# The first block's diagonal as a product with the identity, in a linear-attention and two-layer kernel

## The chip, the cores and the metric

The kernel runs on one NeuronCore of a Trainium2 chip. The metric is the device time of one execution in microseconds (us). The engines are named as in the profile: PE is TensorE (matrix products), PEld its weight loads, DVE is VectorE, ACT is ScalarE, POOL is GpSimd, SP is SyncE, which issues nearly all transfers.

## The reference

```python
def _attn_ref(r, k, v, w, u):            # B, H, S, D = 4, 8, 768, 48
    for t in range(S):
        cur = np.einsum('bhd,bhe->bhde', u[None] * kt, vt)
        y[:, :, t] = np.einsum('bhd,bhde->bhe', rt, state + cur)
        state = w[None, :, :, None] * state + np.einsum('bhd,bhe->bhde', kt, vt)

def _moe_ref(x, w_in, w_out, alpha):      # x is y as (3072, 384); d_ff = 2048
    h = x @ w_in
    g = np.maximum(h, 0.0) + alpha * np.minimum(h, 0.0)
    return g @ w_out

def _moe2_ref(x, w_in, w_out):            # same sizes
    h = x @ w_in
    sp = np.where(h > 20.0, h, np.log1p(np.exp(np.minimum(h, 20.0))))
    return (h * np.tanh(sp)) @ w_out
```

Token t of a sequence sees the decayed state of the tokens before it, and itself through the bonus u: the coefficient of its own v is the sum over d of r·u·k, one number for each head and token.

## The kernel before

The sequence of 768 tokens is cut into six blocks of 128, for each of the four batch entries. Block 0 is worked out in four whole units, 0 to 3, one for each batch entry; there is no state yet, so the output of a unit is (its masked matrix of scores, with the coefficients on the diagonal) times v. The later blocks go in half units with a carried state (units 4 to 23). As soon as block 0 of all four batch entries stands in the tile `x`, the first layer starts: `mA_h s` makes a 128x512 tile h of hidden slot s (9 matrix products of 512 columns, each fp32 factor split into a high and a low part of type fp32r), `mA_g`, `mA_hi`, `mA_lo` make the activation and split it on ACT and DVE, and `mA_out s` adds it to the three output banks (9 more). There are 96 such slots, 16 for each block; a `batch` (the attention of a half unit) is slipped in at every fourth slot or so. The second layer follows with another 96 slots.

The order on every engine is written out: each piece of work is entered with a number of the table `PLACES`, all pieces are sorted by it, and each engine executes its share strictly in that order. An engine that waits for one instruction holds up all behind it. The transfers are issued by SP in the same order, each waiting for the eighth one before it.

The work ahead of slot 0, unit by unit (u is 0 to 3; the tile with r and k is w8u, w10u, w12u, w14u, the one with k and v w9u, w11u, w13u, w15u):

- `m_first` and `prep_rk` (DVE): the product r·k, and r and k scaled by the decay table RK.
- `c_first` (PE, then a copy by ACT into the tile cc): the coefficients.
- `preset_first`: fills the tile A with the coefficients on its diagonals and zeros elsewhere. For units 0, 1 and 2 this is a select on POOL (L439), for unit 3 eight scaled copies of the identity on ACT (L437).
- `scores` (PE, L458): 32 products into two banks "sc", shared by all units. `masked` (DVE, L462): copies the scores that lie above the diagonal into A, one half at a time.
- `attend0` (PE, L473): A times v, into the unit's output bank (yt, acc or h). `x_first` (ACT) and `x_first_lo` (DVE) split the output into the high and the low part of `x`.
- `keep_warm` (PE, L597): products of zeros into a bank that nobody reads; eight at the start and ten single ones between the units.
- `table_Kn` makes a table of decays from RK, `prep_kn` (POOL) scales k by it, `states_first` makes the first state. `half_tables` (POOL) rewrites the mask columns of the constants tile for the half units once block 0 has used them.
- For units 4 and 5: `prep_c` and `prep_c2` make the coefficients (POOL, then a sum on DVE), `prep_pair` (DVE, L382) scales r and k by RKs, which is RK moved by a transfer, `preset` and `masked` fill the matrix Ah.
- `w_scale`, `w_join`, `w_hi`, `w_lo`: unpack a slot's weights (ACT, DVE, ACT, DVE or POOL). Slot 1's high weights go into the tile that RK stands in.

Of the kernel before, what the change touches and what calls it, by code (L numbers as in the profile page):

```python
# [54 lines left out]
def more_state(u):  # L55
# [6 lines left out]
    "load_unit 2": -124.1803, "load_unit 3": -121.8174, "pad_v 1": -119.5623, "m_first 0": -118.998,
    "c_first 0": -117.2355, "dma_start#": -115.5868, "more_raw 3": -115.5854, "memset": -115.5721,
    "load_k 1": -115.4582, "tensor_scalar": -115.426, "dma_start##": -115.3727, "pad_v 0": -115.2759,
    "load_k 2": -115.0763, "load_k 0": -114.1881, "prep_rk 0": -113.5294, "keep_warm 3####": -111.4759,
# [7 lines left out]
    "m_first 3": -99.4133, "load_RKs": -98.9853, "scores 1": -98.8978, "prep_rk 3": -98.7566, "more_raw 7": -97.9969,  # L73
    "preset_first 1": -97.8327, "attend0 0": -97.7559, "preset_first 2": -97.6565, "w_join (0,0)": -97.4588,
    "c_first 3": -97.3694, "masked 1 0": -97.0636, "masked 1 1": -97.0296, "keep_warm 3###": -96.9282,
    "keep_warm 3#########": -96.6439, "w_hi (0,0) False": -96.6418, "prep_kn 1": -96.5019, "keep_warm 3#": -96.4984,
# [983 lines left out]
```

## Time and profile before

| | before |
|---|---|
| median of 3 runs | 872.95 us (871.37 to 873.61) |
| the profiled execution | 871.12 us |
| its span, first to last instruction | 869.4 us |
| granted TensorE clock | 1.000 |
| PE busy | 860.9 us (99%) |
| DVE busy | 631.2 us |
| ACT busy | 616.1 us |
| POOL busy | 103.7 us |

The span is what the trace covers; 1.72 us of the profiled execution lie outside it. Busy times are sums over the span; PE's includes the products of zeros. One slot of the first layer is 18 products of about 0.227 us, 4.08 us.

### The profile page before, as it was taken

The numbers are of one execution on the slowest core, as the hardware profiler recorded it, in microseconds if no ns is written. First come the engines' busy times: TensorE is split into PE (matmuls) and PEld (weight loads), VectorE is DVE, ScalarE is ACT, GpSimd is POOL, SyncE is SP. The second block draws the span as 40 slices with busy tenths as digits, with TensorE's granted clock in tenths as the row PEclk, the third lists the DMA queues.
The fourth block names the chain that finished last, engine by engine and source line by source line (L and its number), as shares of the span: only waits on it lengthen the run. The fifth ranks groups of instructions, "written<-read, shape, count | busy, mean of one in ns | idle before, by whom it ended". The sixth has DMA issues, their size and how long they took to land.

```text
span 869.4 us, 16713 instructions
## 1 busy us (share of the span) xinstructions
PE 860.9 (99%) x6380; PEld 711.8 (82%) x6380; DVE 631.2 (73%) x1013; ACT 616.1 (71%) x1174; POOL 103.7 (12%) x121
## 2 busy tenths in 40 slices
PE   9999999999999999999999999999999999999998
PEld 6777888888888888888888888888888888888897
DVE  7788865657656565554666887887887887887876
ACT  3797755454455545445555998998998998998886
POOL 4744222111122111100002000000000000000000
PEclk9999999999999999999999999999999999999999
DMA  8977455254344426211620300110110110100101
GB/s 316 278 220 213 111 187 147 77 180 152 130 135 141 139 88 214 70 56 64 214 82 31 110 1 1 26 48 1 26 48 1 25 50 0 27 12 1 26 12 37
DMA packets 65840, 80.41 MB, mean 92 GB/s; under 512 B 39712, under 2 KB 52960, under 8 KB 65760
## 3 DMA queue, kind: packets, MB, share of 16 engines
q1 hardware_dynamic: 65200, 79.24, 30.0%
q8 instruction: 50, 0.82, 0.4%
q14 instruction: 30, 0.25, 0.1%
q10 hardware_dynamic: 560, 0.10, 0.1%
HBM read 61.16 MB, written 15.73 MB: 88 GB/s over the span
## 4 chain that ended last, share of the span: by engine, by line
PE 91%; DMA 4%; ACT 2%; SPq 1%; DVE 1%; issue 0%; POOL 0%; ACTq 0%; DVEq 0%; POOLq 0%
PE h L239 43%; PE acc L644 21%; PE sc L765 8%; PE acc L765 8%; PE yt L765 4%; PE acc L763 3%; DMA rk<-in_rkT 1%; DMA wrawr<-in_w 1%; PE sc L763 1%; PE sc L458 1%; PE h L489 1%; DMA w15u<-in_nat 1%; DMA nat<-in_nat 1%; PE yt L510 1%; PE sc L503 1%; PE yt L489 1%
## 5 line engine op out<-in xcount | busy, mean ns | idle before, releaser
L239 PE MATMUL h<-x,w 128*128 128x512 f32 x1728 | 415.9, 390 | 1.9 <-DVE x L164 1.0
L239 PEld LDWEIGHTS h<-x,w 128*128 128x128 f32 x1728 | 323.8, 188 | 71.2 <-DVE w L164 1.7
L644 PE MATMUL acc<-ghi,w 128*128 128x512 f32 x516 | 175.2, 394 | 0.0
L612 ACT ACTIVATE m<-h 128x512 f32<-128x512 f32 x96 | 57.3, 597 | 87.6 <-PE h L239 87.5
L644 PEld LDWEIGHTS acc<-ghi,w 128*128 128x128 f32 x516 | 96.8, 188 | 21.3
L614 DVE SCALAR_TENSOR_TENSOR g<-m,oma,h 128x512 f32<-128x512 f32 x96 | 71.7, 746 | 57.7 <-ACT m L612 56.6
L161 ACT ACTIVATE ghi<-g 128x512 fp32r<-128x512 f32 x86 | 54.3, 631 | 76.1 <-PE acc L644 46.1
L644 PE MATMUL acc<-glo,w 128*128 128x512 f32 x258 | 100.5, 389 | 0.0
L164 DVE TENSOR_TENSOR glo<-g,ghi 128x512 fp32r<-128x512 f32 x86 | 60.2, 701 | 51.8 <-ACT ghi L161 51.7
L702 DVE SCALAR_TENSOR_TENSOR a<-ghi,h 128x512 f32<-128x512 f32 x96 | 66.1, 688 | 37.8 <-ACT ghi L699 31.3
L702 DVE SCALAR_TENSOR_TENSOR g<-s,c 128x512 f32<-128x512 f32 x95 | 66.7, 702 | 22.7 <-ACT s L699 20.7
L710 ACT ACTIVATE m<-h 128x512 f32<-128x512 f32 x96 | 56.4, 588 | 35.0 <-PE h L239 35.0
L164 DVE TENSOR_TENSOR gloB<-g,ghiB 128x512 fp32r<-128x512 f32 x105 | 72.1, 686 | 6.8 <-ACT ghiB L161 6.8
L699 ACT ACTIVATE ghi<-m,biases 128x512 f32<-128x512 f32 x96 | 69.6, 725 | 3.2
L161 ACT ACTIVATE ghiB<-g 128x512 fp32r<-128x512 f32 x105 | 64.8, 617 | 8.8 <-PE acc L644 6.9
L699 ACT ACTIVATE glo<-ghi,biases 128x512 f32<-128x512 f32 x96 | 68.1, 709 | 0.1
L699 ACT ACTIVATE s<-glo,biases 128x512 f32<-128x512 f32 x96 | 68.1, 709 | 0.0
L699 ACT ACTIVATE s<-s,biases 128x512 f32<-128x512 f32 x96 | 68.0, 708 | 0.0
L765 PE MATMUL sc<-ghiB,w 128*128 128x512 f32 x192 | 66.9, 389 | 0.0
L702 DVE SCALAR_TENSOR_TENSOR b<-ghi,a 128x512 f32<-128x512 f32 x96 | 65.8, 685 | 0.1
L702 DVE SCALAR_TENSOR_TENSOR c<-glo,b 128x512 f32<-128x512 f32 x95 | 65.8, 692 | 0.0
L765 PE MATMUL acc<-ghiB,w 128*128 128x512 f32 x192 | 61.7, 389 | 0.0
(185 smaller groups left out, 1156.7 us busy)
## 6 DMA issues: line engine op xcount, KB each, us to landing
wrawr<-in_w SPq DMA_DIRECT2D x28, 768.0 KB, 5.7
nat<-in_nat SPq DMA_DIRECT2D x40, 288.0 KB, 4.3
w2d<-wj SPq DMA_DIRECT2D x16, 384.0 KB, 2.6
wraw<-w2d SPq DMA_DIRECT2D x16, 384.0 KB, 3.0
rk<-in_rkT SPq DMA_DIRECT2D x40, 128.0 KB, 3.0
x2d<-xo SPq DMA_DIRECT2D x6, 768.0 KB, 3.5
x<-x2d SPq DMA_DIRECT2D x6, 768.0 KB, 4.4
rk<-in_rkT SPq DMA_DIRECT2D x40, 96.0 KB, 2.7
```

Of the source, the lines that this page charges most:

```text
L161: act.activation(out=hi, in_=src, func=AF.Copy)
L164: eng.tensor_tensor(out=lo, in0=src, in1=hi.bitcast(F32), op=ALU.subtract)
L239: pe.matmul(h, w_in(layer, f, a, c), x[:, b, c, :], start=(k == 0), stop=(k == 3 * KC - 1))
L489: pe.matmul(y[i][64 * q:64 * q + 64, p * HC:(p + 1) * HC], T[ROWS[h], 2 * bp + i, k, :], pair[i][ROWS[h], 0, k, t], start=(r == 0 and not ...
L612: act.activation(out=m, in_=hA[s], func=AF.Relu, scale=-1.0)
L614: dve.scalar_tensor_tensor(out=g, in0=m, scalar=oma[:, f:f + 1], in1=hA.pop(s), op0=ALU.mult, op1=ALU.add)
L644: pe.matmul(acc[0][c], w_out(0, f, a)[:, c * 128:(c + 1) * 128], g[b], start=(f == 0 and k == 0), stop=(f == NF - 1 and k == 2))
L699: act.activation(out=out, in_=in_, func=AF.Square, scale=scale, bias=fin[bias])
L702: dve.scalar_tensor_tensor(out=out, in0=in0, scalar=scalar, in1=in1, op0=op0, op1=ALU.mult)
L710: act.activation(out=bnew("t", n), in_=v["h", n], func=AF.Tanh, scale=0.5)
L763: pe.matmul(acc[1][t][:, :DM], g[a][:, t * C:(t + 1) * C], w_out(1, f, b), **se)
L765: pe.matmul(acc[1][t], w_out(1, f, a)[:, t * 128:(t + 1) * 128], g[b], **se)
```

## The change

The diagonal no longer stands in A. `scaled_v` multiplies v by the coefficients, head by head, into a free part of the tile that holds k and v: for unit 0 with three instructions on DVE, for units 1, 2 and 3 with eight on ACT (the switches `?va 1` to `?va 3`). `diag_first` adds it to the output bank: three products of 128x128 with the identity, ahead of `attend0`, which now always adds. `zero_A` clears the two tiles A once, on POOL; units 2 and 3 use them again as units 0 and 1 left them, since `masked` writes the same places each time (the switches `?mask` keep `masked` as it was, on DVE). The select on POOL and the copies of the identity on ACT are gone. The table of places is rewritten for everything up to slot 23, so the order of other work changes too; after the first `mA_h` the order of PE is as before. The ten single `keep_warm` are all still there, in other places.

```diff
 PLACES = {
-    "tables": -133.8283, "dma_start": -128.3432, "load_unit 1": -128.1527, "load_unit 0": -125.2362,
+    "tables": -133.8283, "load_unit 1": -129.22293, "dma_start": -128.3432, "load_unit 0": -125.2362,
...
-    def preset_first(u):
-
-        A_t[u] = per.tile([128, 2, NPR, C], F32, tag=f"w{2 + u % 2}", name="A")
-        if other(f"preset {u}"):
-            A = A_t[u].rearrange("s q p t -> s (q p) t")
+    def zero_A(u):
+
+        A_t[u] = A_t[u + 2] = per.tile([128, 2, NPR, C], F32, tag=f"w{2 + u}", name="A")
+        pool.memset(A_t[u], 0.0)
+
+    vc_t = {}
+
+    def scaled_v(u):
+
+        o = vc_t[u] = inp[u][1][:, 0].rearrange("s (c q x) -> s c q x", c=KC, q=2)
+        v, c = inp[u][2], c_t[u][1][:, :, 0]
+        if other(f"va {u}"):
             for h in range(H):
-                act.activation(out=A[:, h], in_=ident, func=AF.Copy, scale=c_t[u][1][:, h])
+                p, q = divmod(h, 2)
+                x = c[:, q * NPR + p:q * NPR + p + 1]
+                to, x0 = (o[:, p, q, 0:D], v[:, h * D:(h + 1) * D]) if p < KC else \
+                    (o[:, :, q, D:64], v[:, h * D:(h + 1) * D].rearrange("s (c e) -> s c e", c=KC))
+                act.activation(out=to, in_=x0, func=AF.Copy, scale=x)
             return
-        pool.affine_select(out=A_t[u].rearrange("s q p t -> s (q p) t"), in_=c_t[u][1].to_broadcast([128, H, C]),
-                           pattern=[[0, H], [-1, C]], compare_op=ALU.is_equal, fill=0.0, base=0, channel_multiplier=1)
+        eng = pool if other(f"vc {u}") else dve
+        by = c.rearrange("s (q p) -> s p q", q=2)
+        eng.tensor_tensor(out=o[:, :, :, 0:D], in0=v[:, 0:2 * KC * D].rearrange("s (p q d) -> s p q d", p=KC, q=2),
+                          in1=by[:, 0:KC].unsqueeze(3).to_broadcast([128, KC, 2, D]), op=ALU.mult)
+        for q in range(2):
+            h = 2 * KC + q
+            eng.tensor_tensor(out=o[:, :, q, D:64], in0=v[:, h * D:(h + 1) * D].rearrange("s (c e) -> s c e", c=KC),
+                              in1=by[:, KC, q:q + 1].unsqueeze(2).to_broadcast([128, KC, 64 - D]), op=ALU.mult)
+
+    def diag_first(u):
+
+        w = vc_t[u].rearrange("s c q x -> s c (q x)")
+        for c in range(KC):
+            pe.matmul(yt_t[u][:, c * C:(c + 1) * C], w[:, c], ident, start=(c == 0), stop=False)
...
-                              start=(p == 3 and c == 0), stop=(p == 2))
+                              start=False, stop=(p == 2))
...
+        for u in range(2):
+            at(-103.33, zero_A, u)
```

On PE, the place where unit 0's output is made, before (sc is unit 1's and unit 2's scores, h the coefficients of unit 3, yt unit 0's output bank, acc with ghi a `keep_warm`):

```order
L458 MATMUL sc<-w10u 64x128 x2
L473 MATMUL yt<-A,w9u 64x128 x6
L473 MATMUL yt<-A,w9u 48x128 x6
L400 MATMUL h<-ut,g 128x2 x4
L597 MATMUL acc_319<-ghi 128x384
L597 MATMUL acc_321<-ghi 128x384
L597 MATMUL acc_326<-ghi 128x384
L458 MATMUL sc<-w12u 64x64 x2
```

The same place on PE in the changed kernel:

```order
L609 MATMUL sc<-w10u 64x128 x2
L528 MATMUL h<-ut,g 128x2 x4
L591 MATMUL yt<-cst,w9u 128x128 x3
L630 MATMUL yt<-A,w9u 64x128 x6
L630 MATMUL yt<-A,w9u 48x128 x6
L754 MATMUL acc_349<-ghi 128x384
L609 MATMUL sc<-w12u 64x64 x2
```

Three products with the identity (cst) stand ahead of unit 0's output, the coefficients of unit 3 moved ahead of it, and two of the three `keep_warm` went elsewhere.

On DVE, the start of units 0 and 1 before (glo, ghi and g are the products r·k of `m_first`, the rows with RK are `prep_rk`):

```order
L392 TENSOR_TENSOR glo<-w8u 112x512
L376 TENSOR_TENSOR w8u<-w8u,RK 112x1024
L392 TENSOR_TENSOR glo<-w10u 112x512
L376 TENSOR_TENSOR w10u<-w10u,RK 112x1024
L462 COPY_PREDICATED A<-cst,sc 128x512
L392 TENSOR_TENSOR ghi<-w12u 112x512
L462 COPY_PREDICATED A<-cst,sc 128x512
L376 TENSOR_TENSOR w12u<-w12u,RK 112x1024
```

The same place on DVE in the changed kernel:

```order
L520 TENSOR_TENSOR glo<-w8u 112x512
L504 TENSOR_TENSOR w8u<-w8u,RK 112x1024
L580 TENSOR_TENSOR w9u<-w9u,cc 128x6x48
L584 TENSOR_TENSOR w9u<-w9u,cc 128x3x16 x2
L619 COPY_PREDICATED A<-cst,sc 128x512
L520 TENSOR_TENSOR glo<-w10u 112x512
L504 TENSOR_TENSOR w10u<-w10u,RK 112x1024
L520 TENSOR_TENSOR ghi<-w12u 112x512
L504 TENSOR_TENSOR w12u<-w12u,RK 112x1024
L619 COPY_PREDICATED A<-cst,sc 128x512
```

The scaling of unit 0's v came in, and the first `masked` of unit 0 moved ahead of unit 1's `m_first`.

On DVE, the end of block 0 and the start of the first layer before (x is `x_first_lo`, cc the sum of `prep_c2`, rk `prep_pair` of unit 4, w and wj are weights, Ah is unit 4's `masked`, g is `mA_g 0`):

```order
L164 TENSOR_TENSOR x<-h,x 128x3x128
L417 TENSOR_REDUCE cc<-nat 128x8
L164 TENSOR_TENSOR x<-acc_229,x 128x3x128
L164 TENSOR_TENSOR x<-yt,x 128x3x128
L164 TENSOR_TENSOR x<-h,x 128x3x128
L382 TENSOR_TENSOR rk<-rk,RKs 112x1024
L164 TENSOR_TENSOR w_453<-wj,w_453 128x768
L193 SCALAR_TENSOR_TENSOR wj<-w6r 128x768
L382 TENSOR_TENSOR rk<-rk,RKs 112x1024
L193 SCALAR_TENSOR_TENSOR wj<-w7r 128x768
L462 COPY_PREDICATED Ah<-cst,sc 128x256
L614 SCALAR_TENSOR_TENSOR g<-m,oma,h 128x512
```

The same place on DVE in the changed kernel:

```order
L292 TENSOR_TENSOR x<-yt,x 128x3x128
L545 TENSOR_REDUCE cc<-nat 128x8
L292 TENSOR_TENSOR x<-acc_240,x 128x3x128
L292 TENSOR_TENSOR x<-h,x 128x3x128 x2
L545 TENSOR_REDUCE cc<-nat 128x8
L510 TENSOR_TENSOR rk<-rk,RKs 112x1024
L292 TENSOR_TENSOR w_485<-wj,w_485 128x768
L321 SCALAR_TENSOR_TENSOR wj<-w6r 128x768
L510 TENSOR_TENSOR rk<-rk,RKs 112x1024
L321 SCALAR_TENSOR_TENSOR wj<-w7r 128x768
L771 SCALAR_TENSOR_TENSOR g<-m,oma,h 128x512
L619 COPY_PREDICATED Ah<-cst,sc 128x256 x2
```

Unit 0's part comes first now, the sum of unit 5's coefficients moved from behind `mA_g 0` to a place ahead of `prep_pair`, and both `masked` of unit 4 stand behind `mA_g 0`.

## Rows read from the trace of the kernel before

**Rows 1.** Waits of PE, 31 to 110 us: total, times, longest (us).

```profile
PE sc L458 <- DVE rk L382: 1.0, 1, 1.0
PE h L239 <- DVE w L164: 0.9, 2, 0.5
PE h L239 <- DVE x L164: 0.8, 1, 0.8
PE h L489 <- DVE g L614: 0.4, 1, 0.4
```

**Rows 2.** Timeline of PE, 8 to 31 us: start, duration, work, instructions.

```profile
8.37 0.96 PE L400 MATMUL yt<-ut,glo 112*128 112x2 f32 x8
9.19 1.86 PE L597 MATMUL acc<-ghi 128*128 128x384 f32 x4
10.98 1.10 PE L458 MATMUL sc<-w8u 48*64 48x128 f32 x32
12.01 0.91 PE L597 MATMUL acc<-ghi 128*128 128x384 f32 x2
12.76 0.95 PE L400 MATMUL acc<-ut,glo 112*128 112x2 f32 x8
...
19.03 2.83 PE L597 MATMUL acc<-ghi 128*128 128x384 f32 x6
21.79 1.10 PE L458 MATMUL sc<-w12u 48*64 48x64 f32 x32
...
26.09 1.91 PE L597 MATMUL acc<-ghi 128*128 128x384 f32 x8
27.93 1.53 PE L473 MATMUL h<-A,w13u 128*64 128x128 f32 x24
29.29 1.48 PE L473 MATMUL h<-A,w15u 128*64 128x128 f32 x24
```

**Rows 3.** Timeline of DVE, 31 to 41 us; in brackets its idle time and releaser.

```profile
31.89 0.55 DVE L164 TENSOR_TENSOR x<-h,x 128x384 fp32r<-128x384 f32 x1
33.20 1.50 DVE L382 TENSOR_TENSOR rk<-rk,RKs 112x1024 f32<-112x1024 f32 x1 [0.76 <-DMA RKs<-RK]
...
36.35 2.05 DVE L382 TENSOR_TENSOR rk<-rk,RKs 112x1024 f32<-112x1024 f32 x1
...
39.64 0.73 DVE L614 SCALAR_TENSOR_TENSOR g<-m,oma,h 128x512 f32<-128x512 f32 x1
```

**Rows 4.** Windows: stretch, its length, busy of PE, PEld, DVE, ACT, POOL, clock, DMA.

```profile
45.00:50.00 5.00, 5.00 (x24) 4.14 (x23) 4.28 (x6) 4.97 (x13) 2.08 (x2) 1.00 0.89 250
```

**Rows 5.** Timeline: the weight loads of the split `keep_warm` (three 128x128 products).

```profile
27.06 0.74 PEld L597 LDWEIGHTS acc<-ghi 128*128 128x128 f32 x6 [0.67 <-PE acc L597]
```

**Rows 6.** Timeline of DVE and POOL, 8 to 28 us.

```profile
8.25 1.22 DVE L376 TENSOR_TENSOR w8u<-w8u,RK 112x1024 f32<-112x1024 f32 x1
...
9.62 1.41 POOL L439 TENSOR_SCALAR_AFFINE_SELECT A<-cc 128x1024 f32<-128x1024 f32 x1 [1.92 <-ACT cc L402]
10.11 1.99 DVE L376 TENSOR_TENSOR w10u<-w10u,RK 112x1024 f32<-112x1024 f32 x1
10.98 0.33 POOL L913 MEMSET w11u<- 128x288 f32 x1
...
12.83 0.67 DVE L392 TENSOR_TENSOR ghi<-w12u 112x512 f32<-112x512 f32 x1
...
15.66 1.16 POOL L439 TENSOR_SCALAR_AFFINE_SELECT A<-cc 128x1024 f32<-128x1024 f32 x1 [4.35 <-ACT cc L402]
15.90 2.00 DVE L376 TENSOR_TENSOR w14u<-w14u,RK 112x1024 f32<-112x1024 f32 x1
...
26.25 1.44 DVE L462 COPY_PREDICATED A<-cst,sc 128x512 f32<-128x512 uint32 x2 [0.18 <-issue]
```

**Rows 7.** Timeline of ACT: four small scaled copies (`preset` of unit 4).

```profile
31.20 1.05 ACT L429 ACTIVATE Ah<-cst,cc 128x64 f32<-128x64 f32 x4
```

**Rows 8.** Timeline of POOL: one of the two products of `prep_c`.

```profile
31.51 1.01 POOL L408 TENSOR_TENSOR nat<-nat,ubt 128x384 f32<-128x384 f32 x1 [0.56 <-POOL cst L265]
```

More of the change, by code (lines that the diff above doesn't have):

```diff
@@ L60 @@
 PLACES = {
-    "tables": -133.8283, "dma_start": -128.3432, "load_unit 1": -128.1527, "load_unit 0": -125.2362,
[L62 to L65, printed above, removed]
@@ L66 @@
-    "<lambda> 0": -111.3741, "scale_Kn": -109.6007, "<lambda> 2": -108.8137, "w_scale (0,0)": -108.7521,
[6 rows of a table removed]
[L73 to L76, printed above, removed]
[7 rows of a table removed]
@@ L84 @@
-    "w_hi (0,1) False": -84.3399, "x_first_lo 0": -84.3204, "states_first 0": -84.1486,
[3 rows of a table removed]
-    "w_hi (0,2) False": -9.0297, "scores 4": -7.6474, "w_join (0,3)": -7.6021, "prep_kn 4": -6.5654,
[4 rows of a table removed]
-    "tables_seat": 1.9613, "mA_out 0": 2.0723, "w_join (0,4)": 2.1732, "mA_hi 1": 2.2917, "w_scale (0,5)": 2.2957,
[8 rows of a table removed]
-    "mA_out 3": 4.8272, "mA_lo 4": 4.9016, "mA_g 5": 4.9113, "batch 5": 4.9611, "w_hi (0,6) False": 5.1766,
-    "w_scale (0,8)": 5.2656, "more_raw 11": 5.4186, "mA_hi 5": 5.4234, "preset 6 0": 5.4724, "t_decay 5": 5.4939,
@@ L104 @@
-    "w_lo (0,6)": 5.5084, "mA_out 4": 5.7163, "w_hi (0,7) True": 5.8446, "mA_h 6": 5.9176, "mA_lo 5": 6.1715,
[3 rows of a table removed]
-    "w_hi (0,8) False": 6.9804, "w_scale (0,10)": 7.0735, "w_hi (0,9) True": 7.2287, "more_raw 13": 7.3665,
[3 rows of a table removed]
-    "w_hi (0,10) False": 8.5586, "batch 6": 8.605, "x_parts 6": 8.6069, "w_scale (0,11)": 8.6193,
[5 rows of a table removed]
-    "w_join (0,12)": 10.7625, "mA_lo 10": 10.8653, "mA_g 11": 10.89, "w_hi (0,12) False": 11.0336,
[4 rows of a table removed]
-    "w_hi (0,13) True": 12.5785, "x_parts 7": 12.6986, "load_unit 9": 12.7519, "mA_hi 12": 12.8252,
@@ L124 @@
-    "w_hi (0,14) False": 12.9398, "mA_out 11": 12.9799, "w_lo (0,14)": 12.9935, "w_lo (0,13)": 13.2622,
-    "w_scale (0,15)": 13.3173, "prep_c 9": 13.3735, "mA_h 13": 13.5197, "mA_h 14": 13.5472, "w_join (0,15)": 13.6724,
-    "w_hi (0,15) True": 13.8183, "load_unit 10": 13.8272, "mA_lo 12": 13.8955, "mA_g 13": 13.9819,
[7 rows of a table removed]
+    "tables": -133.8283, "load_unit 1": -129.22293, "dma_start": -128.3432, "load_unit 0": -125.2362,
+    "m_first 0": -124.39778, "load_unit 2": -124.1803, "load_unit 3": -121.8174, "c_first 0": -120.10369,
@@ new lines @@
+    "prep_rk 0": -118.39482, "scaled_v 0": -117.23539, "pad_v 1": -115.94455, "dma_start#": -115.5868,
+    "memset": -115.5721, "load_k 1": -115.4582, "tensor_scalar": -115.426, "dma_start##": -115.3727,
+    "more_raw 3": -115.28754, "pad_v 0": -115.2759, "load_k 2": -115.0763, "load_k 0": -114.1881,
+    "keep_warm 3####": -111.4759, "<lambda> 0": -111.3741, "scale_Kn": -109.6007, "<lambda> 2": -108.8137,
[7 rows of a table added]
+    "m_first 3": -99.4133, "load_RKs": -98.9853, "keep_warm 3###": -98.9169, "scores 1": -98.8978,
[15 rows of a table added]
@@ new lines @@
+    "mA_h 1": -10.0052, "w_hi (0,2) False": -9.0297, "scores 4": -7.6474, "w_join (0,3)": -7.6021, "mA_g 0": -4.2426,
[7 rows of a table added]
+    "w_hi (0,4) False": 2.6901, "mA_h 2": 2.7398, "w_join (0,5)": 2.88962, "mA_g 2": 2.9067, "w_lo (0,4)": 2.95249,
[8 rows of a table added]
+    "t_decay 5": 5.4939, "w_lo (0,6)": 5.5084, "mA_out 4": 5.7163, "w_hi (0,7) True": 5.8446, "mA_hi 5": 5.90619,
+    "mA_h 6": 5.9176, "prep_c 7": 6.07343, "mA_lo 5": 6.1715, "load_unit 8": 6.21, "preset 6 1": 6.232,
+    "t_update 5": 6.2695, "mA_out 5": 6.4894, "w_scale (0,9)": 6.48947, "w_join (0,8)": 6.4895, "w_lo (0,7)": 6.5889,
@@ L134 @@
+    "x_parts 5": 6.7792, "mA_g 6": 6.78299, "mA_hi 6": 6.7945, "w_join (0,9)": 6.8343, "w_hi (0,9) True": 6.83682,
[4 rows of a table added]
+    "mA_g 8": 8.2832, "more_raw 14": 8.5104, "w_hi (0,10) False": 8.5586, "x_parts 6": 8.6069, "mA_hi 8": 8.61081,
[6 rows of a table added]
+    "w_hi (0,12) False": 11.0336, "prep_kn 7": 11.1115, "mA_hi 11": 11.1167, "w_lo (0,12)": 11.263,
[5 rows of a table added]
+    "x_parts 7": 12.77391, "w_hi (0,14) False": 12.94517, "w_lo (0,14)": 12.96764, "mA_hi 12": 12.97406,
[133 rows of a table added]
 }
@@ L460, in masked @@
     def masked(u, q):
+        if u < B and not other(f"mask {u} {q}"):
+            A = A_t[u][:, q]
+            act.activation(out=A, in_=sc_t[u][q][:, 0:NPR * C].rearrange("s (p t) -> s p t", p=NPR), func=AF.Copy)
+            pool.affine_select(out=A, in_=A, pattern=[[0, NPR], [1, C]], compare_op=ALU.is_gt, fill=0.0, base=0,
+                               channel_multiplier=-1)
+            return
         m, n = (mask, C) if u < B else (mask2, HC)
@@ L924, in attention_and_two_ff @@
             at(E["rk"][u] - 0.001, m_first, u)
-            for work, name in ((prep_rk, "rk"), (c_first, "c"), (pad_v, "pad"), (scores, "sc"), (preset_first, "p"),
+            for work, name in ((prep_rk, "rk"), (c_first, "c"), (pad_v, "pad"), (scores, "sc"), (scaled_v, "p"), (diag_first, "p"),
                                (attend0, "a"), (x_first, "hi"), (x_first_lo, "lo"), (prep_kn, "kn")):
```

235 rows, old and new, of the table PLACES are left out of this document.

## The prediction

> **What bounds the kernel now.** PE is busy nearly throughout, so the time is the products it has to make plus the places where it stands still. I read its waits first, and only from 31 us on, because the first product of the first layer starts at 31.87 and everything from there to the end is the same work in the same order on PE before and after. In 31 to 110 us there are four lines [rows 1], 1.0 + 0.9 + 0.8 + 0.4 = 3.1 us. All lie ahead of 52 us; behind that PE has no wait that the early part could take away. So the change can move two things: when PE reaches the first layer, and how much of these 3.1 us is left.
>
> Next, PE's own timeline ahead of the layer [rows 2]. Each row begins before the modelled end of the one ahead of it: 8.37 + 0.96 is past 9.19, 10.98 + 1.10 past 12.01, 19.03 + 2.83 past 21.79. From the first coefficients at 8.37 to unit 3's `attend0` at 29.29 PE works without a gap: those 20.92 us are its own queue, a good third of it `keep_warm`. That is what the reader must see: POOL's selects and DVE's masks are early enough not to stop PE, so shortening them alone gives nothing.
>
> Third, DVE from 31 to 41 [rows 3]. The last `x_first_lo` runs at 31.89, then DVE stands 0.76 us until the transfer of RKs lands, and `prep_pair` starts at 33.20. From there to `mA_g 0` at 39.64 DVE runs through, and each of PE's waits but the third hangs on a link of this chain (`w_lo` of slot 1, `prep_pair`, `mA_g 0`). So after 31.87 DVE is the bound, with 0.76 us of slack ahead of it. The third wait, for `x` of unit 4 at about 51 us, comes at the end of a stretch in which ACT has no room: 4.97 us busy of 5 [rows 4]. That stretch is started by `mA_g 0`, so it shifts with it.
>
> **The change, part by part.** *The products with the identity.* Four times three, 128x128 in fp32. The trace has the same shape in the split `keep_warm`: its six weight loads (two for each product) take 0.74 us [rows 5] and the products follow them. I take 0.74 us for a unit, 2.96 us in all. From below, `attend0` with its 12 products in pairs takes 29.29 - 27.93 = 1.36 us [rows 2], 0.23 for a step of the same 128 columns, three of them 0.68; from above, one whole `keep_warm` of the same columns in one piece, 0.93 (half of 1.86) [rows 2]. The bounds are 2.7 and 3.7 us. Nothing hides it, since PE has no gap there.
>
> *The keep_warm.* Nine stand between the first coefficients and unit 3's `attend0`, before and after. What one costs depends on its neighbour. Before: a pair 10.98 - 9.19 = 1.79, singles 12.76 - 12.01 = 0.75 and another such, a three 21.79 - 19.03 = 2.76, a whole with a split one 27.93 - 26.09 = 1.84 [rows 2]: 7.89 us. After: five singles and two pairs, 5 x 0.75 + 2 x 1.79 = 7.33. That is 0.56 us less.
>
> *Waits that come in on PE.* The first `masked` of unit 0 now stands ahead of unit 1's `m_first` on DVE. With one `keep_warm` ahead of them, the scores of unit 0 start at 9.19 + 0.75 = 9.94 and end at 11.04; the scaling of v (three small instructions, less than the 1.5 us between 9.5 and there, at 0.67 for 512 elements [rows 6]) is hidden by this. Then 0.72 for a mask (half of 1.44), 0.67 for `m_first` [rows 6], and two handovers of 0.1: PE gets unit 1's coefficients at 12.7. It would be ready after the scores (12.01 - 10.98 = 1.03 [rows 2]), `table_Kn` (four products, an estimate of 0.5 from two steps of 0.23 for 128 columns) and a `keep_warm`, at 12.2. Wait 0.5. Unit 2's `m_first` comes 1.22 + 0.67 later, 14.6, and PE is ready at 14.25. Wait 0.4. Later units have DVE ahead of PE.
>
> *POOL's selects out, a clearing in.* The two selects that run beside `prep_rk` cost DVE something: 1.99 and 2.00 us for what takes 1.22 alone [rows 6]. With them gone DVE gains 0.77 twice, already used in the 12.7 and 14.6 above. The clearing of A lies at about 8 to 10 us, beside unit 0's `prep_rk`, and the question is whether it costs the same 0.77. The rows say no: unit 1's `prep_rk` ran beside 0.92 us of select and then 0.33 us of clearing, unit 3's beside 0.92 us of select alone, and they took 1.99 and 2.00. I cost it at nothing; if it did block, unit 0's scores would begin at 10.2 and all behind them 0.3 us later. The Trainium skill (SBUF — State Buffer, "Who interferes with whom") has it so too: a VectorE instruction with two inputs in SBUF contends with a GpSimd instruction that reads SBUF, not with one that only writes.
>
> *ACT.* 24 small scaled copies come in, 8 go. Four of 128x64 take 1.05 [rows 7], so eight of 48 columns or fewer about 2.1 us; the three groups end near 19.5, 23.5 and 26.5, and PE wants them near 23, 30 and 28. From 3.5 us ahead (unit 1) to 1.3 us (unit 3). Hidden; if ACT were 2 us later, unit 3's would show.
>
> So unit 3's `attend0` starts at 29.29 + 2.96 - 0.56 + 0.9, less 0.2 for smaller seams: 32.4, that is 3.1 us later. It ends at 33.9, its high part at 34.4, and `x_first_lo` of unit 3 runs at 34.45, where it ran at 31.89 [rows 3]: only 2.55 later, because before it queued behind the other three and now they are done.
>
> *SP.* Unit 1's first load now goes ahead of the constants, and two loads of 192 KB (unit 1's k, the bonus) ahead of the weights of slots 0 to 2. Unit 0's r and k keep their fifth place, and the same bytes as before stand ahead of RKs, so both land as they did. The weights land a little later; the slot 0 weights are first used at the first product of the layer, some 20 us behind.
>
> *The order behind it.* DVE's 0.76 us wait for RKs is gone, since the transfer's landing does not depend on PE. That gives 0.76 back. But the sum of unit 5's coefficients now stands ahead of `prep_pair`: about 0.45 by its 384 elements, as many as `x_first_lo` has with 0.55 less the overlap of two neighbours, and it waits for `prep_c 5` on POOL. POOL must first do `half_tables` (three small copies, an estimate of 0.8 from the 1.01 of a full product), which waits for the last mask of unit 3 (ends about 28.6), then `prep_c 4`, `prep_kn` twice, `prep_c 5`: six products of about 1.01 to 1.03 [rows 8], so 28.6 + 0.8 + 6.15 = 35.55. `prep_pair` then starts at 36.0 instead of 33.20, 2.8 later; without POOL's wait it would be 35.4. From there to `mA_g 0` the chain is the same, less the mask that stood ahead of it (0.35, half of the 0.72 for twice the columns): `mA_g 0` at 42.05 instead of 39.64. Queued behind that are unit 4's `batch` on PE and the full stretch on ACT, and both keep their length. The four waits of rows 1 stay, one by one, much as they are: PE arrives later, but so does DVE.
>
> **Sum.** 2.4 us later at `mA_g 0`, and from there nothing gives it back: 871.12 + 2.4 = 873.5 for the profiled execution. The median shown is 1.83 us above that execution, so on the median's footing 872.95 + 2.4 = 875.35. About 0.3%, 2.6 us, is what a measurement of this kernel can tell from no change; 2.4 us is just inside.
>
> **The rivals.** *A: as worked out,* 874 to 877, chance 55%. Half of it lies inside 0.3% and nearly half beyond.
>
> *B: PE's extra work is mostly hidden.* If the products with the identity cost 2.7 us or less, DVE's small waits don't come (0.9) and POOL finishes `prep_c 5` in time (0.6), `mA_g 0` is late by 2.4 - 0.25 - 0.9 - 0.6, about 0.7. Time 873 to 874. For it: RKs sets a floor at 33.2 that PE does not move. Against it: PE without a gap. 20%.
>
> *C: slower by clearly more.* The place is DVE's sum of unit 5's coefficients. Everything of the first layer's start stands behind it, and it hangs on six POOL products. POOL's products beside two-input DVE work can take much longer than 1 us (DVE's own price beside POOL is 2.05 against 1.50 for `prep_pair` [rows 3]). If `prep_c 5` ends 1 us later, the sum starts 1 us later, and so does everything; it decides from 35.0 on, when the last `x_first_lo` is done. A wait from the new order of slots 4 to 23 would add to it. 2.4 + 1 to 2.4 + 2.6: 876.4 to 878. 17%.
>
> *D: faster.* It would need the selects to have been what PE waited for, directly or through the masks. Then the first layer would start earlier, and with all 3.1 us of rows 1 gone as well the time would be about 869.8. For it: POOL's selects and DVE's masks do get out of each other's way. Against it: PE's rows without a gap, with the same ten `keep_warm`. 8%.
>
> **How the numbers follow.** The predicted time is A's, 875.3. The range leaves out D, and takes in B and C and the scatter of the runs: 871.8 to 878.2. Faster by over 0.3% is D: 0.07. Slower by over 0.3% is C and a little under half of A: 0.43. Within 0.3%: 0.50.
>
> **What would show it.** PE's timeline: three products with the identity at 0.74 us a unit, no gap but two small ones ahead of the coefficients of units 1 and 2, unit 3's `attend0` at 32.4. DVE: `prep_rk` at 1.22 in all four units; `prep_pair` at 36.0 with POOL as the releaser of the sum ahead of it, not RKs; `mA_g 0` at 42.0. PE's waits behind 31 us about 3 us as before, then none. It is wrong if PE reaches unit 3's `attend0` before 31 us (then the identity products or the `keep_warm` are cheaper than their rows), if the sum of unit 5 does not wait for POOL, or if the loss of 2.4 us at 42 us is smaller or larger at 110 us, where the new order of slots 4 to 23 would have acted.

## The result, and the profile after

The changed kernel is slower: 877.52 us (875.09 to 883.44, 6 runs) against 872.14 (870.40 to 873.61, 6 runs), ratio 1.0072 with a 95% interval of 1.0052 to 1.0092 (a ratio, here and below, is not that of the two medians, which is 1.0062 here). That is 5.4 us where 2.4 were forecast. The time lies inside the range, but a change within 0.3% was held the likeliest outcome, and this one is 0.6 to 0.7%. In 4 of the 6 runs the mean granted clock was .998 or .988 and not 1.000; the profiled execution, 875.09 us, is one at 1.000 and the lowest of the six. So the traces show 4.0 of the 5.4 us (875.09 less 871.12).

From the page of the changed kernel, the engines' busy times over its span of 873.3 us:

```profile
PE 864.9 (99%) x6404; PEld 715.2 (82%) x6404; DVE 630.8 (72%) x1016; ACT 618.6 (71%) x1190; POOL 98.6 (11%) x120
```

PE's waits from 31 to 130 us in the changed kernel, where [rows 1] stood:

```profile
PE h L367 <- DMA x<-y: 1.4, 1, 1.4
PE h L367 <- DVE x L292: 0.7, 1, 0.7
PE h L367 <- DVE w L292: 0.5, 1, 0.5
PE sc L609 <- DVE Ah L619: 0.2, 1, 0.2
```

The waits for `prep_pair` (1.0) and `mA_g 0` (0.4) are gone and the others are smaller; the first line is new. It lies at about 110 us, behind the stretch in which I had looked for a cost.

PE's timeline of the changed kernel from the first coefficients to unit 3's `attend0`, against [rows 2] (L528 coefficients, L591 the identity products, L630 `attend0`):

```profile
9.40 0.95 PE L528 MATMUL yt<-ut,glo 112*128 112x2 f32 x8
...
13.62 1.05 PE L528 MATMUL acc<-ut,glo 112*128 112x2 f32 x8 [0.29 <-DVE glo L520]
...
20.13 0.91 PE L591 MATMUL yt<-cst,w9u 128*128 128x128 f32 x6
20.98 1.53 PE L630 MATMUL yt<-A,w9u 128*64 128x128 f32 x24
...
24.32 0.94 PE L591 MATMUL acc<-cst,w11u 128*128 128x128 f32 x6
25.18 1.53 PE L630 MATMUL acc<-A,w11u 128*64 128x128 f32 x24
...
29.19 0.83 PE L591 MATMUL h<-cst,w15u 128*128 128x128 f32 x6
29.86 1.78 PE L754 MATMUL acc<-ghi 128*128 128x384 f32 x4
31.48 0.83 PE L591 MATMUL h<-cst,w13u 128*128 128x128 f32 x6
32.24 1.53 PE L630 MATMUL h<-A,w13u 128*64 128x128 f32 x24
33.60 1.48 PE L630 MATMUL h<-A,w15u 128*64 128x128 f32 x24
```

From start to start the identity products take 0.85, 0.86, 0.67 and 0.76 us, 3.14 in all. From the first coefficients to unit 3's `attend0` are 24.20 us, where 20.92 were: +3.28. All of it starts 1.03 us later.

DVE at the start of units 0 to 2 (L520 `m_first`, L504 `prep_rk`), then from the last `x_first_lo` to `mA_g 0`, against [rows 6] and [rows 3]:

```profile
8.53 0.69 DVE L520 TENSOR_TENSOR glo<-w8u 112x512 f32<-112x512 f32 x1 [2.57 <-DMA w8u<-in_rkT]
9.26 1.22 DVE L504 TENSOR_TENSOR w8u<-w8u,RK 112x1024 f32<-112x1024 f32 x1
...
13.60 1.23 DVE L504 TENSOR_TENSOR w10u<-w10u,RK 112x1024 f32<-112x1024 f32 x1
...
35.20 1.01 DVE L292 TENSOR_TENSOR x<-h,x 128x384 fp32r<-128x384 f32 x2
37.04 0.56 DVE L545 TENSOR_REDUCE cc<-nat 128x8 f32<-128x384 f32 x1 [0.83 <-POOL nat L537]
37.51 1.67 DVE L510 TENSOR_TENSOR rk<-rk,RKs 112x1024 f32<-112x1024 f32 x1
...
40.83 1.22 DVE L510 TENSOR_TENSOR rk<-rk,RKs 112x1024 f32<-112x1024 f32 x1
...
42.84 0.74 DVE L771 SCALAR_TENSOR_TENSOR g<-m,oma,h 128x512 f32<-128x512 f32 x1
```

POOL's timeline, the clearing of A (L562) and then the same stretch (L391 is `half_tables`, L537 the second product of `prep_c 5`):

```profile
7.58 1.84 POOL L562 MEMSET A<- 128x1024 f32 x2
...
29.97 0.23 POOL L391 COPY cst<-cst 64x64 f32<-64x64 f32 x1 [5.36 <-DVE A L619]
...
36.00 1.00 POOL L537 TENSOR_TENSOR nat<-nat 128x384 f32<-128x384 f32 x1
```

So the sum of unit 5's coefficients waits for POOL, as worked out, and RKs is not waited for. `mA_g 0` is 3.20 us later than before: 1.03 by the start and 2.17 by the rest.

SP's timeline from 98 to 109 us, of the changed kernel and then of the kernel before:

```profile
98.01 5.84 SPq L400 DMA_DIRECT2D rk<-in_rkT  x8
103.96 1.17 SPq L423 DMA_DIRECT2D nat<-in_nat  x2
105.24 3.87 SPq L739 DMA_DIRECT2D x<-y  x6
```

```profile
97.51 3.78 SPq L582 DMA_DIRECT2D x<-y  x6
101.40 1.17 SPq L295 DMA_DIRECT2D nat<-in_nat  x2
102.66 5.15 SPq L272 DMA_DIRECT2D rk<-in_rkT  x8
```

`load_unit 10` went from place 13.83 to 12.75 and stands ahead of `x_parts 7` now, so the six transfers that bring the attention's output into `x` are issued 7.7 us later, and PE waits 1.4 us for them. POOL's order changed with it: `prep_c` of unit 10 now stands ahead of that of unit 9, so POOL's 9.0 us wait there (until 109.4 us, 106.7 before) is for unit 10's load, where it was for unit 9's.

### The profile page after: what moved, and what is told of

Its sections match the earlier page's. It is cut to its first block, busy times and chain, and to the rows that moved or that the text cites. A ratio compares the mean times of both kernels' runs of the same rounds, so it can differ in the third digit from the quotient of the medians.

```text
span 873.3 us, 16769 instructions
## 1 busy us (share of the span) xinstructions
PE 864.9 (99%) x6404; PEld 715.2 (82%) x6404; DVE 630.8 (72%) x1016; ACT 618.6 (71%) x1190; POOL 98.6 (11%) x120
## 4 chain that ended last, share of the span: by engine, by line
PE 93%; SPq 1%; DVE 1%; ACT 0%; DMA 0%; issue 0%; POOL 0%; POOLq 0%; ACTq 0%
PE h L367 44%; PE acc L801 22%; PE sc L922 7%; PE acc L922 7%; PE yt L922 4%; PE acc L920 3%; PE sc L609 1%; PE sc L920 1%; PE h L646 1%; PE yt L667 1%; PE sc L660 1%; PE yt L646 1%; SPq L400 1%; SPq L739 0%; DMA x<-y 0%; PE h L667 0%
```

## The experiments

All times are medians; each ratio is to runs of the kernel before on the same chip (871.29 us for the first four, 871.36 for the next four, 870.67 for the g kernels, 871.47 for the h kernels). "Late" is the sum of PE's waits behind 62 us in the profiled execution (0.8 before, 1.7 after).

| kernel | us | ratio (95%) | profiled | `mA_g 0` | late |
|---|---|---|---|---|---|
| e1_load | 876.62 | 1.0072 (1.0054 to 1.0089) | 876.84 | 42.83 | 2.9 |
| e2_sum | 881.51 | 1.0118 (1.0084 to 1.0151) | 882.74 | 47.58 | 3.6 |
| e3_sp | 886.39 | 1.0185 (1.0150 to 1.0221) | 892.76 | 51.61 | 8.7 |
| e4_nodiag | 875.93 | 1.0065 (1.0040 to 1.0091) | 876.26 | 41.24 | 3.6 |
| f1_warm10 | 877.40 | 1.0068 (1.0051 to 1.0085) | 875.86 | 43.20 | 1.8 |
| f2_before6 | 870.94 | 1.0002 (0.9988 to 1.0016) | 871.75 | 39.56 | 0.8 |
| f3_warm10_old | 875.39 | 1.0043 (1.0027 to 1.0059) | 874.46 | 43.45 | 0.5 |
| f4_before_load | 871.61 | 1.0003 (0.9994 to 1.0013) | 873.41 | 40.98 | 1.2 |
| g3_newmath | 872.59 | 1.0021 (1.0013 to 1.0030) | 873.70 | 42.39 | 0.7 |
| g4_newmath_4less | 870.81 | 1.0004 (0.9996 to 1.0013) | 870.25 | 39.26 | 0.5 |
| g5_before_4less | 870.75 | 1.0006 (0.9998 to 1.0015) | 870.06 | 39.36 | 0.5 |
| g1_4less | 876.64 | 1.0063 (1.0041 to 1.0084) | 875.30 | 42.67 | 0.9 |
| h1_4less_RKs | 871.39 | 0.9992 (0.9971 to 1.0014) | 870.57 | 39.57 | 0.5 |
| h2_newmath_slots | 875.05 | 1.0036 (1.0024 to 1.0049) | 876.49 | 41.63 | 3.5 |

Profiled time less `mA_g 0` less late is 830.2 to 831.7 in all rows but e3_sp (832.4), and some 830.6 before and after alike. So, to within 1.5 us, two numbers say all: when the layer's first activation starts, and what PE waits behind 62 us. The late waits are 0.5 to 1.2 us in the kernels with the old order of the slots, and 1.7 to 3.6 in those with the new one (8.7 in e3_sp).

**The arithmetic alone, g3_newmath.** The order of before in every place, with only the new pieces put in where the old ones stood:

```diff
-    "preset_first 0": -103.1898, "attend0 0": -97.7559,
+    "zero_A 0": -103.33, "zero_A 1": -103.33, "scaled_v 0": -103.1898, "diag_first 0": -97.7564, "attend0 0": -97.7559,
```

> The kernel before with its whole order, its loads and its eight first keep_warm matmuls left, and only the arithmetic changed: the scaled copies of v at the places where the diagonal was laid down, the identity products just ahead of the first product of each of the four units, A cleared once. Theory 1 (the arithmetic costs what it puts into TensorE's queue, the late load and the new order of the slots cost the rest): attend0 of unit 3 starts near 32.3 (29.29 before), x_first_lo 3 and the sum of unit 5 follow, prep_pair 4 0 starts near 35.4 (33.20 before) with no wait for RKs left, mA_g 0 near 41.8 (39.64), nothing new behind 62 us, so the median is 1.9 to 2.4 us above the kernel before: 873.2 to 873.8. Rival (the identity products are hidden, and the whole cost of the change lies in its order): within 0.7 us of the kernel before.

1.9 us slower than its own before, at the edge of what was expected. PE's and DVE's timelines of this kernel:

```profile
32.83 0.94 PE L736 MATMUL h<-cst,w15u 128*128 128x128 f32 x6
33.70 1.53 PE L775 MATMUL h<-A,w15u 128*64 128x128 f32 x24
```

```profile
36.27 1.22 DVE L655 TENSOR_TENSOR rk<-rk,RKs 112x1024 f32<-112x1024 f32 x1
```

Unit 3's `attend0` is 24.28 us behind the first coefficients (9.42 in this execution): +3.36. `prep_pair` starts without a wait: the 0.76 us that DVE stood for RKs before are used up, so that much of PE's extra queue costs nothing. Theory 1 holds.

**Pay for the products with keep_warm, g4_newmath_4less and g5_before_4less.** Four single `keep_warm` left out of g3_newmath, and of the kernel before:

```diff
-            at(place, keep_warm, 1, other(f"warm {n}"))
+            at(place, keep_warm, 0 if n in (0, 1, 3, 5) else 1, other(f"warm {n}"))
```

> The kernel of g3_newmath with four of the single keep_warm matmuls between the units left out (they compute nothing that is used), some 0.74 to 0.93 us of TensorE's queue each. Theory 1: TensorE's queue sets the end of the first 35 us, so the 3.0 to 3.7 us taken out of it pay for the identity products: mA_g 0 is back near 39.6 to 40.2, prep_pair 4 0 near 33.2, where it waits again for RKs, and the median is 871.0 to 872.0. Rival 1 (the chain on VectorE and GpSimd sets the end, not TensorE's queue): mA_g 0 stays over 41, the median within 0.5 us of g3_newmath. Rival 2 (fewer keep_warm matmuls lower the granted clock): the clock of some runs is .995 or less, and the median is over that of g3_newmath.

> The kernel before with the same four keep_warm matmuls left out. Theory 1: TensorE is 3 us earlier at attend0 of unit 3, but prep_pair 4 0 waits for RKs (0.76 us of wait before, at 33.20), so it can start 0 to 0.8 us earlier at most: the median is 870.5 to 871.3 where the kernel before has 871.3. Rival 1 (TensorE's queue sets the end there too): 868.5 to 869.5. Rival 2 (fewer keep_warm matmuls lower the granted clock): the clock of some runs is .995 or less, and the median is over the kernel before.

In the new arithmetic the four are worth 1.8 us (872.59 to 870.81) and `mA_g 0` comes at 39.26: PE's queue set the end, as theory 1 says (the median is a little under its range). In the kernel before they are worth nothing: unit 3's `attend0` starts at 27.08, but RKs has not landed. The granted clock was .998 or .997 in 7 of the 11 runs of g5_before_4less, which could hide a gain; but its four runs at .999 or more, 870.06 to 872.06, are no faster than the kernel before either, to within 0.2 us. DVE in g5_before_4less:

```profile
32.83 1.59 DVE L639 TENSOR_TENSOR rk<-rk,RKs 112x1024 f32<-112x1024 f32 x1 [1.43 <-DMA RKs<-RK]
...
36.08 2.04 DVE L639 TENSOR_TENSOR rk<-rk,RKs 112x1024 f32<-112x1024 f32 x1
```

**RKs earlier, h1_4less_RKs.** g5_before_4less with

```diff
-    "load_RKs": -98.9853,
+    "load_RKs": -104.95,
```

> The kernel of g5_before_4less (the kernel before with four keep_warm matmuls fewer) with the load of RKs put ahead of unit 5's v, k and nat load, so that it is issued 1.2 us earlier. Theory 1 (after TensorE's queue is shortened the only thing in front of prep_pair 4 0 is the landing of RKs, a wait of 1.4 us there): prep_pair 4 0 starts near 31.7 (32.83), mA_g 0 near 38.3 (39.36), the median is 869.5 to 870.2, some 1 us under the kernel before. Rival (something else is late there by then, the sums on VectorE or the rest of unit 4's data): prep_pair 4 0 starts within 0.3 us of 32.83, the median 870.5 to 871.0.

The wait went, and in the profiled execution the gain went with it. DVE's timeline, then POOL's:

```profile
31.70 1.22 DVE L639 TENSOR_TENSOR rk<-rk,RKs 112x1024 f32<-112x1024 f32 x1
33.37 1.33 DVE L421 TENSOR_TENSOR w<-wj,w 128x768 fp32r<-128x768 f32 x1 [0.45 <-ACT w L418]
34.62 1.76 DVE L450 SCALAR_TENSOR_TENSOR wj<-w6r 128x768 uint32<-128x768 uint32 x1
36.30 2.04 DVE L639 TENSOR_TENSOR rk<-rk,RKs 112x1024 f32<-112x1024 f32 x1
```

```profile
32.88 1.00 POOL L665 TENSOR_TENSOR nat<-nat,ubt 128x384 f32<-128x384 f32 x1 [1.38 <-DMA nat<-in_nat]
33.96 1.60 POOL L666 TENSOR_TENSOR nat<-nat 128x384 f32<-128x384 f32 x1
```

The 1.13 us gained at `prep_pair` are given back in the next two rows: 0.45 of waiting for ACT, and 1.33 and 1.76 us for what took 0.94 each in g5_before_4less, beside POOL's products, which are late by unit 5's load and stretched in turn. So `prep_pair` came early, as theory 1 has it, and `mA_g 0` did not (39.57). Of the time this settles less: the granted clock was .998 or less in 10 of the 12 runs, the profiled one too, and the two at .999 or more, 869.79 and 869.96, lie in theory 1's range and below all runs of the kernel before beside them (870.00 at the least). Whether an earlier RKs gains at the full clock is open. By medians no version here beats the kernel before.

**The new order of the slots alone, h2_newmath_slots.** g3_newmath with the changed kernel's places from slot 2 on, of which one line is

```diff
-    "x_parts 7": 12.6986, "load_unit 9": 12.7519, "load_unit 10": 13.8272,
+    "load_unit 9": 12.7519, "load_unit 10": 12.75259, "x_parts 7": 12.77391,
```

> The kernel of g3_newmath (old order, new arithmetic) with the places from slot 2 on taken from the changed kernel, the load of units 6 apart. Theory 1 (the new order of the slots costs by its waits behind 60 us, whatever the start): mA_g 0 as in g3_newmath (42.0 to 42.4), the wait of TensorE for x from y, 1.2 to 1.4 us, near 110 us is there, and the median is 1.0 to 2.0 us above g3_newmath: 873.6 to 874.6, with a granted clock of .999 or more in all runs. Rival 1 (that wait only comes with the late start of the changed kernel): within 0.5 us of g3_newmath's 872.59. Rival 2 (the new order of the slots lowers the granted clock by itself): runs at .996 or less, and the median over 875.

2.5 us over g3_newmath (1.7 when each is taken against its own before). PE's waits behind 62 us in h2_newmath_slots (in g3_newmath there are three, of 0.3, 0.2 and 0.2 us):

```profile
PE h L1194 <- DVE g L1598: 1.0, 1, 1.0
PE h L1194 <- DMA x<-y: 0.9, 1, 0.9
PE acc L1628 <- DVE glo L1119: 0.7, 1, 0.7
PE h L1194 <- DVE w L1119: 0.6, 1, 0.6
...
```

All 12 runs had a clock of .999 or more. So the new order costs by waits of its own, with an early start too; the transfer is only one of four. The profiled execution is the slowest of the twelve, so its 3.5 us may be more than the usual. Rival 1 falls. Theory 1 holds in direction: its 1.0 to 2.0 us are met against each kernel's own before and passed by the medians, and the transfer costs 0.9, not 1.2 to 1.4.

**The same from the other side, f1_warm10 and f3_warm10_old.** The changed kernel with ten first `keep_warm` for eight, and that with the places of before from slot 2 on:

```diff
+    "?first b": 1,
```

> The changed kernel with ten products of zeros at the start instead of eight. Theory (the falls of the granted clock come from PE's pause ahead of the first coefficients, which in the changed kernel wait for unit 0's later load): with two more, PE has work until 10 to 11.3 us, past the landing, so there is no pause; the granted clock is 0.999 or more in at least five of six runs, and the time is that of the changed kernel at full clock plus 0.6 to 1.9 us, 875.5 to 878, with a spread under 2.5. Rival (the falls come from the products with the identity or from the new places of the single products of zeros): falls to 0.998 and below stay in half of the runs, and the spread stays at 5 us or more.

> The changed kernel with ten products of zeros at the start and with the places of the kernel before for all work from slot 2 on. Theory (the new order of the slots costs PE one wait of 1.4 us for the transfers into x, and gave nothing back): the wait at 110 us goes, no wait over 0.4 us is left behind 62 us, and the span is 0.9 to 1.4 us under that of the changed kernel with ten. Rival (the wait is the late start carried on, since PE arrives later than the order was made for): a wait of 1 us or more stays between 62 and 130 us, and the time is the same within 0.5 us.

2.0 us between the two, 877.40 and 875.39, all runs at .999 or more. Behind 62 us PE waits only 0.5 us in f3_warm10_old, in two places, though it starts late (first coefficients at 10.00): the waits belong to the new order and not to the late start.

Two more `keep_warm` took the lower clocks away, but not the time: the first coefficients came at 9.74 in f1_warm10.

**One line of the new order put back, e3_sp.**

```diff
-    "x_parts 7": 12.77391,
+    "x_parts 7": 12.6986,
```

> The changed kernel with unit 7's x_parts put ahead of the loads of units 9 and 10 again, so that SP issues the six transfers into x ahead of ten loads that wait for PE. Theory: PE's 1.4 us wait for these transfers at 110 us goes; span 871.9. Rival (the wait only moves to the next thing that is late, the first slots of block 1): the wait for the transfers goes and another of 0.7 us or more comes up within 10 us behind it; span 872.8 or more.

A miss. The wait for x from y went, and a larger one came:

```profile
PE yt L646 <- POOL T L650: 6.2, 2, 5.8
```

POOL's timeline there (the first products of `prep_c` of units 10 and 9), then SP's (unit 9's load, and the end of unit 10's):

```profile
128.20 0.99 POOL L536 TENSOR_TENSOR nat<-nat,ubt 128x384 f32<-128x384 f32 x1 [16.42 <-DMA nat<-in_nat]
...
130.22 0.99 POOL L536 TENSOR_TENSOR nat<-nat,ubt 128x384 f32<-128x384 f32 x1
```

```profile
111.58 3.77 SPq L739 DMA_DIRECT2D x<-y  x6
115.46 1.31 SPq L423 DMA_DIRECT2D nat<-in_nat  x2
...
122.07 2.20 SPq L423 DMA_DIRECT2D nat<-in_nat  x2
```

Unit 10's load now stands behind the six transfers and unit 9's load. POOL, whose order still has unit 10 first, stands 16.4 us for it (9.0 in the changed kernel) and clears T for the next `batch` only behind the products of both units. With this order on POOL either order of the transfers makes PE wait; the kernel before, which has unit 9 first and the clearing ahead of unit 10, had no wait of either kind over 0.3 us. All six runs had a clock of .996 or less, so the 15 us are not split into waits and clock.

**The late load, e1_load and f4_before_load.** Unit 1's load put back behind the constants in the changed kernel, and put ahead of them in the kernel before:

```diff
-    "load_unit 1": -129.22293,
+    "load_unit 1": -128.1527,
```

> The changed kernel with one number of the table put back, so that SP issues the constants ahead of unit 1's r and k again. In the changed kernel unit 0's r and k land 1.0 us later (5.9 us after issue, 4.8 before) and PE starts the first coefficients at 9.40 instead of 8.37. Theory (PE's queue has no gap, delays add up): first coefficients back at 8.4 to 8.6, unit 3's attend0 at 32.6 instead of 33.60, mA_g 0 at 41.9 instead of 42.9, span 872.3. Rival (the late landing is contention with other loads, whatever the order, or POOL's chain ahead of prep_pair sets the end): first coefficients stay at 9.2 or later, or they come back and mA_g 0 stays within 0.3 of 42.9; span 873.3.

> The kernel before with one number of the table changed: unit 1's two loads ahead of the constants, as in the changed kernel. Nothing else moves. Theory: unit 0's r and k land at 8.4 to 8.8 instead of 7.5, the first coefficients start at 9.3 to 9.6, PE pauses 0.5 us or more where its eight products of zeros ended early, the clock falls in half of the runs or more; time 1 us longer at full clock and 3 to 10 us longer where it falls. Rival (the late landing is nothing the order of the loads causes, or it is hidden behind the products of zeros): time within 0.7 us of before, clock 0.999 or more.

In e1_load unit 0's r and k landed 1.06 us earlier again, and the first coefficients still came at 9.38: the eight first `keep_warm`, which took 8.31 us there, held them. The time did not move. In f4_before_load r and k came 1.44 us later than before (`m_first` at 8.97) and the median 0.3 us, not told from zero; 3 of 12 runs had a clock of .998 or .997, fewer than the half expected.

**The sum moved back behind mA_g 0, e2_sum.**

```diff
-    "prep_c2 5": -77.16975,
+    "prep_c2 5": -0.8142,
```

> The changed kernel with the sum of unit 5's coefficients (a DVE reduce) put back behind mA_g 0. Theory: prep_pair no longer stands behind a sum that waits 0.83 us for POOL; it starts when the last x_first_lo is done, 36.2 instead of 37.51, and mA_g 0 comes at 41.6 to 41.9 instead of 42.9; span 872.1 to 872.4. Rival (POOL's products beside prep_pair now slow it, or PE is the bound there and not DVE): prep_pair starts early but takes 2 us or more, and mA_g 0 or unit 4's batch (43.63) gain under 0.4; span 873 or more.

DVE in e2_sum, where the clock was low and PE some 5 us late:

```profile
41.11 1.97 DVE L510 TENSOR_TENSOR rk<-rk,RKs 112x1024 f32<-112x1024 f32 x1
...
44.74 2.04 DVE L510 TENSOR_TENSOR rk<-rk,RKs 112x1024 f32<-112x1024 f32 x1
```

The 0.83 us of waiting is gone, but both `prep_pair` now run beside POOL's products, 1.97 and 2.04 us for 1.67 and 1.22. From unit 3's `attend0` to the first `batch` it is 9.79 us against 10.03, a gain of 0.24: the rival holds in this execution.

**The diagonal left out, e4_nodiag.** The identity products are gone and `attend0` starts the bank as before; block 0's diagonal is missing from the output.

```diff
-            pe.matmul(yt_t[u][:, c * C:(c + 1) * C], w[:, c], ident, start=(c == 0), stop=False)
```

> The changed kernel without the products with the identity on PE; the scaling of v stays. The diagonal is left out of the output of block 0. Theory: they took 0.85, 0.86, 0.67 and 0.76 us on PE, which has no gap there, so unit 3's attend0 starts 2.9 to 3.1 us earlier (30.6), and the masks of unit 3 and with them POOL's chain 1.7 us earlier; prep_pair and mA_g 0 gain the smaller of the two, about 1.7; span 871.6. Rival (PE's products are not what delays the layer, the loads and POOL are): mA_g 0 gains under 0.7; span 872.7 or more.

Unit 3's `attend0` came 2.64 us earlier, but `mA_g 0` only 1.6, because the sum then waited longer for POOL. PE had 3.6 us of late waits, 1.7 of them for x from y. Mechanism as expected; in time it shows nothing beyond the scatter, with 5 of 9 runs at .998 or less.

**The pause and the clock, f2_before6 and g1_4less.** The kernel before with six first `keep_warm`; and f3_warm10_old with eight, with the load put back and four single ones left out:

```diff
-        keep_warm(8)
+        keep_warm(6)
```

> The kernel before with six products of zeros at the start instead of eight, nothing else. Theory of the pause: PE runs out of work at about 6.3 to 7.1 us, the first coefficients are ready at 8.3, and the granted clock falls for some us afterwards in most runs; mean clock under 0.998 in most runs, time 3 to 20 us longer than before. Rival (the kernel before is not sensitive to this, and the falls belong to the changed part): clock 0.999 to 1.000 in all runs, time within 1.5 us of before.

> The changed kernel with unit 1's loads back behind the constants, eight first keep_warm matmuls, four of the single ones left out, and from slot 2 on the order of the kernel before (f3_warm10_old with the loads put back and six keep_warm fewer). Theory 1 (GpSimd's chain of masks, tables and coefficients, which ended the sum's wait after the change, binds as soon as TensorE's queue is shorter): the sum of unit 5 waits for GpSimd till near 36, mA_g 0 starts near 42.0, and the median is 873.0 to 874.0. Rival (TensorE's queue alone binds): mA_g 0 near 40.5 or earlier, the median 871.5 to 872.3. Falls of the granted clock would put runs over either.

f2_before6 did not move. PE stood 1.53 us ahead of the first coefficients and `attend0` of unit 3 came 0.42 later, but `prep_pair` started at 33.08 (33.20 before), with 0.22 us of idle time where 0.76 were; the clock was 1.000 in 11 of 12 runs, so the rival holds but for one run (.992, 876.15 us). In g1_4less `mA_g 0` came at 42.67, with the sum 2.2 us behind POOL as theory 1 has it, but the clock was .990 to .998 in 5 of 6 runs and low in parts of the first 45 us of the profiled one, and the median tells more of that than of the theory. Its two runs of least time are 872.99 and 873.22.

## Why the prediction was wrong

*PE's queue*: right in its sum, partly by luck. +3.1 forecast, +3.28 measured, +3.36 in g3_newmath. The identity products took 3.14 and not 2.96, and the new places of the `keep_warm` saved 0.30 and not 0.56; of the two small waits 0.29 came, not 0.9, which made up for it.

*DVE's selects and the clearing*: right. `prep_rk` takes 1.22 to 1.23 in every unit. The clearing (7.58 to 9.42 on POOL) meets unit 0's for 0.16 us only, but it covers the whole of unit 0's product r·k, which took 0.69, as against 0.67 to 0.69 in the other units. This agrees with the Trainium skill (SBUF — State Buffer, "Who interferes with whom"): a GpSimd instruction that only writes did not slow VectorE. The other half of that rule shows in e2_sum and h1_4less_RKs, where products that read slowed VectorE. Which side pays is not the same each time: in g5_before_4less two weight instructions of VectorE kept their 0.94 us beside a product of POOL, and that product took 3.74 us for 1.00.

*The chain to `mA_g 0`*: right in its links, its length partly by luck. RKs gave 0.76 back, the sum waited for POOL. 2.41 forecast, 2.17 measured from the first coefficients on. `prep_pair` started 0.5 us later than forecast, counted from there (28.11 for 27.63), and the rest "is the same, less the mask" only in its order: it took 5.33 us and not 6.05, since the two `prep_pair` took 1.67 and 1.22 for 1.50 and 2.05.

*"The four waits of rows 1 stay"*: wrong. The waits for `prep_pair` and `mA_g 0` went, and one of the two for w, 0.34 us, lay at 85.7 us all along and not "ahead of 52 us". It gave nothing back: from `mA_g 0` to unit 4's `batch` are 0.79 us before and after.

*"From there nothing gives it back", and PE "the same work in the same order" behind 31.87*: this is the step that failed. The order on PE is the same, that on SP, DVE and POOL is not. I read PE's waits of the old order, carried them over to the new one and put the new order of the slots at nothing in the sum; it has one sentence in rival C. It costs 2.0 us (f1_warm10 less f3_warm10_old), 1.7 to 2.5 (h2_newmath_slots less g3_newmath), in waits at places where the old order had none or shorter ones.

*"both land as they did"*: wrong. Unit 0's r and k land 1 us later: their first reader starts at 8.37 to 8.97 us in the seven traces with unit 1's load ahead of the constants, at 7.29 to 7.95 in the nine with it behind. But this step alone has no measured price (e1_load, f4_before_load).

*The sum*: 5.4 us, each kernel against its own before, is 1.9 for the arithmetic (g3_newmath), 1.7 for the slots (h2_newmath_slots: 3.6), and 1.8 that came with the changed kernel's places up to slot 2 (1.0 if the slots are taken at 2.5; by the ratios of the table the three parts are 1.8, 1.3 and 3.1). Two readings narrow the last part. e1_load, with the load put back and 5 of 6 runs at .999 or more, is still 5.3 us over its own before. f3_warm10_old and g3_newmath differ in the places up to slot 2 and in two first `keep_warm`; they are 2.1 us apart, each against its own before, with all runs at .999 or more. So neither the load nor the lower clock is needed for it. The traces show 0.5 of it: from the first coefficients to `mA_g 0` are 33.44 us after and 33.45 in f3_warm10_old, 32.97 in g3_newmath and 31.27 before. Where the rest of it arises stays open.

## What to carry to other kernels

That a wait is absent in the old order says nothing of a new one: go through every transfer that changes its place in the issuing queue, however far from the edit, and ask who waits for it last, and which other engine's order now wants it earlier. When a queue without a gap meets a floor (RKs here), a loss on the queue costs only the excess over the slack, and a gain on it buys nothing: taking some 3.5 us of work out of the kernel before moved it by nothing, out of the changed arithmetic by 1.8. Test a bundle of arithmetic and order by putting the arithmetic into the old order first.
